# Attention, soft mixture of experts and MLP on one core: narrowing behind the copies, two pieces later, a reordered table of steps

## The chip, the cores and the metric

The kernel runs on one core of a Trainium2 chip. The metric is the device time of one launch in microseconds (us). Inputs lie in HBM: q, k, v of 4 batches, 12 heads, 448 positions and 64 channels; the experts' weights w1 and w2 (8 experts, 768 by 1024 and 1024 by 768, float32: 6.3 MB an expert); the weights w_in and w_out of the last MLP, which are float64 (768 by 2048 and 2048 by 768, 12.6 MB each).

## What is computed

```python
q_n, k_n = rmsnorm(q, g_q), rmsnorm(k, g_k)                 # per head
attn = softmax(q_n @ k_n.T / 8); x = attn @ v               # -> x: 1792 tokens x 768
logits = x @ phi                                            # 1792 x 32 slots, 4 slots per expert
d = softmax(logits, axis=0); slot_input = d.T @ x           # over tokens: 32 slots x 768
h = maximum(slot_input[e] @ w1[e], 0); slot_out[e] = h @ w2[e]      # 8 experts
c = softmax(logits, axis=1); x = c @ slot_out               # over slots, back to 1792 tokens
h = x @ w_in; g = maximum(h, 0) + alpha * minimum(h, 0); out = g @ w_out
```

## The kernel before, in words

**Attention** (to about 303 us). Two heads make a pair; 24 pairs are worked one behind the other with their steps interleaved. For each pair q and k are loaded, normed, split into two f16 parts, transposed on TensorE (L745) and copied out by ScalarE (L752). Four small transfers on SP's queue then arrange them: L754 and L756 copy k's and q's low parts into kB and qB, `twin` (L761) copies q's upper half over its lower one ("q<-q"), and L773 puts the negated row maximum into a row of qB ("qB<-mr"). `rowmax_mm` (L800) needs q before `twin` overwrites it; `score_mm` (L818) needs all four. ScalarE takes exp (L832, L834, L839), VectorE or GpSimd forms the low part (L850), and the matmuls of L868 and L878 multiply by v. In between, weights are fetched: "unit" is a buffer of 1.5 MB that holds half an expert's w1 or w2, or a raw piece of w_in; `pf` is the queue of such fetches (256 KB transfers at L475, 512 KB at L484), `cv` the queue of steps that narrow w_in from float64 to float32. All of it is 2374 steps in a list. A planner's due times do not set their order here: the table `ORDER` of 2374 numbers does (`plan = [plan[i] for i in ORDER]`, L1195). Each engine runs its own instructions in that order; SP's queue too is in order, a transfer that waits holds all behind it.

**Experts** (to about 417 us). For each expert e: its slot rows times w1[e] (L1339), a copy (`h_sb`, ScalarE, L1350), eight transposes (L1353), two short VectorE operations that write `hT` (L1355, L1361), then hT times w2[e] into the accumulators pS (L1370). In experts 2 to 5 `turn_c(e - 2)` follows: VectorE copies a batch's slot weights cN into `cs` (L1262), GpSimd forms their low part (L1263), TensorE transposes (L1267), ScalarE copies to cT4 (L1270). Expert 3 turns `alpha` ahead of that (L1252 to L1254).

The last 8 of w_in's 16 pieces are not yet narrowed when attention ends. `narrow_in(n)` does one: an absolute value on ScalarE (L540) and five VectorE operations (L541 to L551). `NARROW` says behind which expert which pieces stand.

The weights come as 32 units in a ring of 11 buffers, on SP's queue, w1 then w2 of each expert. Behind the 26th unit SP holds two transfers of w_out (`rawo` 0 and 1, L1281, 1.5 MB each, two pieces of w_out in each); they take the buffers of the two units of w2[5]. The last six units stand behind them. w_out's 16 pieces are widened by `wide_out(f)`: an absolute value (L498), four VectorE operations (L500 to L510), a cast to whi (ScalarE, L1301), a difference to wlo (VectorE, L1303). Pieces 0 to 3 are done early, in expert 6, by `go_early`; `EARLY_STEPS` is the order of their seven steps each. Behind piece 3 SP fetches `rawo` 5, then 2 and 3.

**Last MLP** (to the end). pS is copied out (`s_sb`, L1396: one half by VectorE, the other by ScalarE), turned and multiplied by w_in (L1402, L1414, L1442), and then TensorE runs three matmuls for each part of g times w_out (L1528 to L1530).

Of the kernel before, what the change touches and what calls it, by code (L numbers as in the profile page):

```python
# [353 lines left out]
def fused_attention_softmoe_mlp(  # L354
# [960 lines left out]
    def go_early():  # L1315
        for f in EARLY_STEPS:
            next(early[f], None)
# [5 lines left out]
    for e in range(E):  # L1323
# [38 lines left out]
        if e == E - 2:  # L1362
            go_early()
# [269 lines left out]
```

## Time and profile before

| | |
|---|---|
| median of 3 runs | 685.01 us (684.3 to 691.0) |
| the profiled execution | 685.3 us, span 683.3 us |
| TensorE busy | 616.2 us (90% of the span), mean granted clock 0.975 |
| VectorE, ScalarE, GpSimd busy | 464.9, 372.4, 191.6 us |
| HBM read | 92.18 MB |

The profile's span runs from the first to the last instruction; what lies around it is 2.0 us here. A busy TensorE is not one at its peak: matmuls are pipelined and their ends are modelled, so the waits and the distances between starts say more than the share.

### The profile page before, as it was taken

Reading aid. Unit: us, or ns where it says so; the run is one execution under the profiler, and the core shown is the slowest. Engines: PE = TensorE matmul, PEld = TensorE weight load, DVE = VectorE, ACT = ScalarE, POOL = GpSimd, SP = SyncE. Lnnn points to the kernel's source line nnn. Section 1 sums busy time; section 2 is a strip of 40 time slices with the busy share of each in tenths; the row PEclk is TensorE's granted clock in tenths of the full one; section 3 lists DMA queues with packets and bytes.
Section 4 is the critical chain, followed back from the end, with each engine's and each line's share of the span. In section 5 each row is a group of like instructions: output and inputs, shape, how many; then the busy total and the mean of one; then the engine's idle time right before and its main releaser. Section 6 shows DMA issues by size and latency. Waiting matters only on the chain.

```text
span 683.3 us, 14166 instructions
## 1 busy us (share of the span) xinstructions
PE 616.2 (90%) x5670; PEld 475.9 (70%) x5670; DVE 464.9 (68%) x921; ACT 372.4 (54%) x717; POOL 191.6 (28%) x203
## 2 busy tenths in 40 slices
PE   0799998989999999998868668999999999999997
PEld 0367665666667777764323214888899999999997
DVE  5788999998789877735941444999964545454540
ACT  3799998889999998742321223776521111111110
POOL 6976666557657764111001000000000000000000
PEclk9999999999999999999988969999999999999999
DMA  4575677364456325499999799130020101010101
GB/s 138 133 239 165 188 211 204 110 189 126 131 143 200 99 76 171 123 350 391 425 424 395 283 423 400 67 120 0 1 93 1 47 1 47 1 47 0 47 1 46
DMA packets 36240, 106.89 MB, mean 156 GB/s; under 512 B 5448, under 2 KB 22352, under 8 KB 31824
## 3 DMA queue, kind: packets, MB, share of 16 engines
q1 hardware_dynamic: 36176, 106.01, 44.7%
q8 instruction: 44, 0.72, 0.5%
q14 instruction: 20, 0.16, 0.1%
HBM read 92.18 MB, written 5.51 MB: 143 GB/s over the span
## 4 chain that ended last, share of the span: by engine, by line
PE 63%; ACT 14%; DMA 9%; DVE 8%; POOL 4%; issue 2%; SPq 1%; ACTq 0%; POOLq 0%; DVEq 0%
PE psa L1530 12%; PE psa L1529 12%; PE psa L1528 11%; PE psn L818 5%; DMA unit<-in_moe_w_dram 4%; PE psv L878 4%; PE psv L868 3%; PE psa L1339 3%; ACT e L834 3%; PE psr L800 2%; DMA q<-q 2%; ACT psn L839 2%; POOL nf L717 2%; PE psa L1370 2%; ACT sp L723 1%
## 5 line engine op out<-in xcount | busy, mean ns | idle before, releaser
L1528 PE MATMUL psa<-whi,gh 128*128 128x384 f32 (+1 forms) x448 | 152.0, 339 | 0.0
L1529 PE MATMUL psa<-wlo,gh 128*128 128x384 f32 (+1 forms) x448 | 151.1, 337 | 0.0
L1530 PE MATMUL psa<-whi,gl 128*128 128x384 f32 (+1 forms) x448 | 150.8, 337 | 0.0
L809 DVE TENSOR_REDUCE m<-psr 128x1 f16<-128x448 f32 x168 | 97.7, 615 | 4.8 <-PE psr L800 4.6
L1497 ACT CAST gh<-t 128x512 fp32r<-128x512 f32 x40 | 24.9, 621 | 123.0 <-DVE t L1494 122.5
L1529 PEld LDWEIGHTS psa<-wlo,gh 128*128 128x128 f32 x448 | 84.2, 188 | 2.7
L1528 PEld LDWEIGHTS psa<-whi,gh 128*128 128x128 f32 x448 | 84.2, 188 | 2.7
L1530 PEld LDWEIGHTS psa<-whi,gl 128*128 128x128 f32 x448 | 84.1, 188 | 2.8
L878 PE MATMUL psv<-vH,e 128*128 128x65 f16 (+1 forms) x1152 | 84.2, 194 | 0.0
L878 PEld LDWEIGHTS <-e 128*128 128x128 f16 (+1 forms) x1728 | 79.3, 106 | 0.0
L1491 DVE TENSOR_SCALAR t<-pst,alpha_t 128x256 f32<-128x256 f32 x80 | 34.9, 476 | 62.9 <-PE pst L1485 62.9
L868 PEld LDWEIGHTS psv<-vR,e 128*128 128x128 f32 (+1 forms) x384 | 58.9, 176 | 20.0 <-issue 10.8
L878 PE MATMUL psv<-vL,e 128*128 128x64 f16 (+1 forms) x576 | 72.5, 193 | 0.0
L850 POOL TENSOR_TENSOR e<-ef,e 128x448 f16<-128x448 f32 x48 | 52.0, 1083 | 72.2 <-ACT ef L839 52.7
L868 PE MATMUL psv<-vR,e 128*128 128x65 f32 (+1 forms) x384 | 69.8, 263 | 0.2 <-PE psn L818 0.2
L834 ACT ACTIVATE e<-psn 128x448 f16<-128x448 f32 x120 | 65.2, 544 | 7.5 <-PE psn L818 6.2
L818 PE MATMUL psn<-q,k 128*128 128x448 f16 (+1 forms) x192 | 61.4, 361 | 7.3 <-DMA q<-q 2.0
L818 PE MATMUL psn<-qB,kB 67*128 67x448 f16 (+1 forms) x192 | 61.0, 357 | 1.6 <-DMA qB<-mr 1.4
L800 PE MATMUL psr<-k,q 128*128 128x448 f16 (+1 forms) x192 | 57.2, 374 | 3.5 <-ACT k L752 2.8
L850 DVE TENSOR_TENSOR e<-psn,e 128x448 f16<-128x448 f32 x72 | 44.4, 617 | 21.4 <-ACT psn L839 21.2
L730 POOL TENSOR_TENSOR sp<-nf,sp 128x448 f16<-128x448 f32 x48 | 49.8, 1047 | 12.2 <-ACT sp L723 11.8
L745 PE MATMUL pst<-ident,sp 128*128 128x128 f16 x336 | 27.7, 230 | 17.4 <-POOL sp L730 17.4
(178 smaller groups left out, 1091.2 us busy)
## 6 DMA issues: line engine op xcount, KB each, us to landing
unit<-in_moe_w_dram SPq DMA_DIRECT2D x26, 1536.0 KB, 12.2
unit<-in_moe_w_in_dram SPq DMA_DIRECT2D x24, 512.0 KB, 6.8
rawo<-in_moe_w_out_dram SPq DMA_DIRECT2D x8, 1536.0 KB, 13.2
unit<-in_moe_w_dram SPq DMA_DIRECT2D x36, 256.0 KB, 4.9
qk<-in_q_dram SPq DMA_DIRECT2D x12, 448.0 KB, 3.8
qk<-in_k_dram SPq DMA_DIRECT2D x12, 448.0 KB, 5.4
out_dram<-osb SPq DMA_DIRECT2D x14, 384.0 KB, 2.3
vR<-in_v_dram SPq DMA_DIRECT2D x24, 128.0 KB, 3.8
```

The source lines that it names most:

```text
L730: eng.tensor_tensor(out=d["sp"][:, a, :, D:], in0=d["nf"][:, a], in1=d["sp"][:, a, :, 0:D], op=ALU.subtract)
L800: nc.tensor.matmul(pn[o0:o1, :S], d["q"][:, c0 : c0 + o1 - o0], d["k"][:, h * S : (h + 1) * S], start=True, stop=True)
L809: nc.vector.tensor_reduce(out=d["m"][:, c : c + 1], in_=d.pop(("pn", c))[:, :S], axis=AX.X, op=ALU.max)
L818: nc.tensor.matmul(pe[o0:o1, :S], lhs[:, c0 : c0 + o1 - o0], rhs[:, h * S : (h + 1) * S], start=st_, stop=not st_,)
L834: nc.scalar.activation(e2[:, 0], pe[:, :S], AF.Exp, scale=0.125)
L850: eng.tensor_tensor(out=e2[:, 1], in0=ef, in1=e2[:, 0], op=ALU.subtract)
L868: nc.tensor.matmul(pv[o0:o1, slot, :], d["e", c][:, qs], d["vv"][:, h, sl * D : 4 * D + 1], start=(j == 0), stop=False,)
L878: nc.tensor.matmul(pv[o0:o1, slot, 0:wd], d["e", c][:, w // 2, qs], (vl if w == 1 else vh)[:, 4 * h + sl, 0:wd], start=(j == 0 and w == 0) ...
L1491: nc.vector.tensor_scalar(out=t0[:, cs], in0=ph[:, cs], scalar1=0.0, scalar2=alpha_t[:, f // 2, i : i + 1], op0=ALU.min, op1=ALU.mult)
L1528: nc.tensor.matmul(a, gh[f][:, ms], hi[:, hs], start=(f == 0 and not (packed and m % 2 == 1 and hf == 0)), stop=False)
L1529: nc.tensor.matmul(a, gh[f][:, ms], lo[:, hs], start=False, stop=False)
L1530: nc.tensor.matmul(a, gl[f][:, ms], hi[:, hs], start=False, stop=(f == KF - 1 and not (packed and m % 2 == 0 and hf == 1)))
```

## The change

Three things. The narrowing of w_in's pieces stands behind `turn_c` and not ahead of the second matmuls, and piece 15 goes from expert 3 to expert 4. `EARLY_STEPS` is in two parts, one in expert 6, one in expert 7: pieces 0 and 1 and the start of 2 in the first, the rest of 2 and all of 3 in the second. The table `ORDER` is another one from its 500th step on, which is the fifth pair's; it holds the same 2374 steps.

```diff
@@ ORDER, from its 500th number on
-    244, 1462, 2002, 2003, 1655, 268, 222, 318, 292, 2198, 52, 1679, 1227, 364, 978, 1084, 438, 1607, 923, 2199, 2200,
...
+    244, 1462, 2002, 1679, 558, 2198, 268, 1227, 364, 1829, 1486, 1251, 222, 1607, 318, 582, 2199, 1084, 1132, 978,
...
@@ -1310,16 +1310,19 @@
-    EARLY_STEPS = [0, 1, 0, 0, 0, 0, 0, 2, 1, 1, 1, 1, 0, 1, 3, 2, 2, 2, 2, 1, 2, 3, 3, 3, 3, 2, 3, 3]
-
-    def go_early():
-        for f in EARLY_STEPS:
+    EARLY_STEPS = (
+        (0, 1, 0, 0, 0, 0, 1, 1, 1, 1, 0, 0, 2, 1, 1, 2, 2, 2, 2),
+        (2, 3, 2, 3, 3, 3, 3, 3, 3),
+    )
+
+    def go_early(part):
+        for f in EARLY_STEPS[part]:
             next(early[f], None)
...
-    NARROW = ((8, 9), (10, 11), (12, 13), (14, 15), (), (), (), ())
+    NARROW = ((8, 9), (10, 11), (12, 13), (14,), (15,), (), (), ())
...
@@ -1359,10 +1362,8 @@
-        if e == E - 2:
-            go_early()
-        for n in NARROW[e]:
-            narrow_in(n)
+        if e >= E - 2:
+            go_early(e - E + 2)
         for u in range(2):
             wu = loaded[1, e, u].rearrange("p (t f) -> p t f", t=4)
...
         if 2 <= e < 2 + B:
             turn_c(e - 2)
+        for n in NARROW[e]:
+            narrow_in(n)
```

Three lines are added above the experts' code, so what was L1339 is L1342 in the changed kernel, L1350 and L1353 are L1353 and L1356, L1355 is L1358, L1396 is L1399.

What the change moves, in the engines' own order. On VectorE at the end of expert 2, the kernel before (the second of the two pieces, the casts of cN, then expert 3's hT; L1262 is the cast that `turn_c` waits for):

```order
L541 TENSOR_SCALAR wf<-wf 128x768
L543 CAST wb<-low 128x768
L545 TENSOR_SCALAR wf<-wf 128x768
L548 SCALAR_TENSOR_TENSOR wf<-wb,wf 128x768
L551 SCALAR_TENSOR_TENSOR win_4271<-win_4271,wf 128x768
L1262 CAST cs<-cN 128x4x32 x2
L1355 TENSOR_REDUCE hT<-pst 128x4x4
```

The same place in the changed kernel (expert 2's hT, the casts, then the first of the two pieces):

```order
L1358 TENSOR_REDUCE hT<-pst 128x4x4
L1364 TENSOR_SCALAR hT<-hT 128x4x4
L1262 CAST cs<-cN 128x4x32 x2
L541 TENSOR_SCALAR wf<-wf 128x768
L543 CAST wb<-low 128x768
L545 TENSOR_SCALAR wf<-wf 128x768
L548 SCALAR_TENSOR_TENSOR wf<-wb,wf 128x768
L551 SCALAR_TENSOR_TENSOR win_4231<-win_4231,wf 128x768
```

The casts come ahead of the narrowing, and the narrowing now stands ahead of the next expert's hT. On ScalarE, the absolute values move behind `turn_c`'s copy in the same way.

On VectorE in expert 7, the kernel before (the end of w_out's piece 3, the differences of pieces 2 and 3, then hT; L1396 is the copy of pS with which the last MLP begins):

```order
L506 SCALAR_TENSOR_TENSOR wf<-rawo,wf 128x768
L510 SCALAR_TENSOR_TENSOR wf<-rawo,wf 128x768
L1303 TENSOR_TENSOR wlo<-wf,whi 128x768 x2
L1355 TENSOR_REDUCE hT<-pst 128x4x4
L1361 TENSOR_SCALAR hT<-hT 128x4x4
L1355 TENSOR_REDUCE hT<-pst 128x4x4
L1361 TENSOR_SCALAR hT<-hT 128x4x4
L1396 COPY s_sb<-psa 128x384
```

The same place in the changed kernel (from the second half of hT on; L1399 is that copy):

```order
L1358 TENSOR_REDUCE hT<-pst 128x4x4
L1364 TENSOR_SCALAR hT<-hT 128x4x4
L1303 TENSOR_TENSOR wlo<-wf,whi 128x768
L500 TENSOR_SCALAR wf<-wf 128x768
L502 TENSOR_SCALAR wf<-wf 128x768
L506 SCALAR_TENSOR_TENSOR wf<-rawo,wf 128x768
L510 SCALAR_TENSOR_TENSOR wf<-rawo,wf 128x768
L1303 TENSOR_TENSOR wlo<-wf,whi 128x768
L1399 COPY s_sb<-psa 128x384
```

Expert 7's hT was behind all four pieces, and so was its h_sb on ScalarE, behind their casts (L1301). Now piece 2's cast and difference and all of piece 3 stand behind hT and ahead of s_sb.

On SP's queue at the end of attention, before (qB_117 belongs to the last pair):

```order
L773 DMA qB_115<-mr 1x7x128
L475 DMA unit<-in_moe_w_dram 128x512
L761 DMA q<-q 64x896
L773 DMA qB_117<-mr 1x7x128
L475 DMA unit<-in_moe_w_dram 128x512 x12
```

and now:

```order
L773 DMA qB_115<-mr 1x7x128
L659 DMA vR_124<-in_v_dram 64x2x256
L475 DMA unit<-in_moe_w_dram 128x512 x10
L761 DMA q<-q 64x896
L475 DMA unit<-in_moe_w_dram 128x512
L773 DMA qB_117<-mr 1x7x128
L475 DMA unit<-in_moe_w_dram 128x512
```

The last pair's `twin` had one 256 KB transfer between itself and the pair's before it; it now has ten.

## Rows read from the trace of the kernel before

**Rows 1.** Windows: us, busy us (instructions) by engine, granted clock, DMA share, GB/s.
```profile
90.00:303.00 213.00, 203.07 (x2727) 149.14 (x2726) 174.28 (x363) 188.35 (x391) 121.33 (x120) 1.00 0.54 158
320.00:340.00 20.00, 18.37 (x164) 7.35 (x163) 18.98 (x38) 6.77 (x10) 0.00 (x0) 1.00 1.01 428
480.00:520.00 40.00, 40.00 (x232) 37.15 (x232) 28.56 (x48) 14.16 (x24) 0.00 (x0) 1.00 0.11 40
```

**Rows 2.** Windows around the hole in the transfers, same columns.
```profile
374.00:376.00 2.00, 2.00 (x22) 0.59 (x15) 0.00 (x0) 0.58 (x1) 0.00 (x0) 1.00 0.33 131
...
374.00:382.00 8.00, 7.95 (x72) 3.29 (x68) 1.06 (x6) 1.75 (x3) 0.88 (x2) 1.00 0.21 56
```

**Rows 3.** Waits of SP's queue, 370 to 386: total us, times, longest.
```profile
SPq L1281 <- PE psa L1370: 15.4, 2, 14.5
```

**Rows 4.** Timeline, experts 0 to 2: start, us, engine, line, idle before and releaser.
```profile
320.84 0.55 DVE L541 TENSOR_SCALAR wf<-wf 128x768 f32<-128x768 f32 x1
...
326.77 0.96 DVE L551 SCALAR_TENSOR_TENSOR win<-win,wf 128x768 uint32<-128x768 uint32 x1
...
335.73 2.79 PE L1370 MATMUL psa<-unit,hT 128*32 128x384 f32 x32
...
344.29 1.20 PE L1267 MATMUL pst<-ident,cs 128*128 128x128 f32 x4 [5.77 <-POOL cs L1263]
```

**Rows 5.** Timeline, experts 3 to 6.
```profile
345.42 6.03 PE L1339 MATMUL psa<-unit,slT 128*32 128x512 f32 x24
345.52 0.97 ACT L1270 CAST cT<-pst 128x448 fp32r<-128x448 f32 x1 [5.98 <-PE pst L1267]
...
360.09 0.17 DVE L1253 COPY alpha_t<-pst 128x16 f32<-128x16 f32 x1
...
362.82 5.86 PE L1339 MATMUL psa<-unit,slT 128*32 128x512 f32 x24
...
369.40 0.22 DVE L1355 TENSOR_REDUCE hT<-pst 128x16 f32<-128x64 f32 x1 [8.66 <-PE pst L1353]
...
370.09 2.79 PE L1370 MATMUL psa<-unit,hT 128*32 128x384 f32 x32
...
373.49 3.62 PE L1339 MATMUL psa<-unit,slT 128*32 128x512 f32 x24
...
378.51 2.79 PE L1370 MATMUL psa<-unit,hT 128*32 128x384 f32 x32
...
380.07 1.62 SPq L1281 DMA_DIRECT2D rawo<-in_moe_w_out_dram  x2
```

**Rows 6.** Timeline, expert 7 and the copy behind it.
```profile
405.98 1.91 PE L1339 MATMUL psa<-unit,slT 128*32 128x512 f32 x12 [0.97 <-DMA unit<-in_moe_w_dram]
...
407.59 0.56 DVE L500 TENSOR_SCALAR wf<-wf 128x768 f32<-128x768 f32 x1 [0.99 <-ACT wf L498]
...
409.77 0.96 DVE L510 SCALAR_TENSOR_TENSOR wf<-rawo,wf 128x768 uint32<-128x768 uint32 x1
410.65 1.94 DVE L1303 TENSOR_TENSOR wlo<-wf,whi 128x768 fp32r<-128x768 f32 x2
410.76 0.83 ACT L1301 CAST whi<-wf 128x768 fp32r<-128x768 f32 x1 [2.48 <-DVE wf L510]
411.50 1.07 ACT L1350 COPY h_sb<-psa 128x512 f32<-128x512 f32 x2
...
412.13 1.98 PE L1353 MATMUL pst<-ident,h_sb 128*128 128x128 f32 x8 [4.24 <-ACT h_sb L1350]
...
416.79 0.56 DVE L1396 COPY s_sb<-psa 128x384 f32<-128x384 f32 x1 [2.20 <-PE psa L1370]
```

**Rows 7.** Window at expert 7's transposes, columns as in group 1.
```profile
412.00:414.00 2.00, 1.87 (x8) 1.58 (x8) 0.98 (x3) 0.57 (x2) 0.00 (x0) 0.50 0.96 406
```

**Rows 8.** Timeline, first widening step of w_out's piece 4.
```profile
428.29 0.92 ACT L498 ACTIVATE wf<-rawo 128x768 f32<-128x768 f32 x1
```

**Rows 9.** Waits of TensorE in attention, 90 to 303: total us, times, longest.
```profile
PE psn L818 <- DMA q<-q: 1.6, 1, 1.6
```

184 rows, old and new, of the table ORDER are left out of this document.

## The prediction, before the changed kernel was run

> **What bounds the kernel now.** I read the windows by stage first, then the waits of SP's queue, then the timeline of the experts, where the change's second and third parts lie. From 428 us on TensorE has no gap (40.00 of 40 us in 480 to 520 [rows 1]), so the last MLP is a block that ends earlier by as much as it begins earlier. Ahead of it the experts' stage runs at the rate of the transfers: a DMA share of 1.01 at 428 GB/s [rows 1], by which a 1.5 MB piece takes 3.7 us. But there is one hole. The share is 0.33 in 374 to 376, so the queues run dry at 374.7, and 0.21 over 374 to 382 [rows 2]: 8 x 0.79 = 6.3 us lost. SP waited there, 15.4 us in all, for expert 5's L1370 [rows 3], whose weights' buffers the two pieces of w_out take; six pieces of the experts' weights stand behind these two. They were issued at 380.07, 1.56 us after that L1370 began at 378.51 [rows 5], and began to flow some 0.9 us later (a share of 0.21 over 8 us is 1.7 us of work: 0.7 ahead of the hole, the rest from 381.0 on). So the hole ends when TensorE has reached expert 5's second matmuls, and TensorE is late there: it idles 5.77 us ahead of `turn_c` in expert 2 [rows 4], because the casts of cN stand behind two narrowed pieces on VectorE, and again in expert 3; L1339 then takes 6.03 and 5.86 us where it takes 3.62 in expert 5 [rows 5].
>
> **Part 1, the narrowing behind the copies.** I walk TensorE from expert 2's L1370, at 335.73 [rows 4]. Where nothing waits, L1370 to the next expert's L1339 takes 373.49 - 370.09 = 3.4 us with `turn_c` in it, and L1339 to its own L1370 takes 378.51 - 373.49 = 5.0 [rows 5].
> - Expert 3's L1339: 335.7 + 3.4 = 339.1, not 345.42.
> - Behind it ScalarE runs L1270 (0.97, beginning 0.1 after L1339 [rows 5]) and the absolute value (another pass over 128x768, for which I take the cast's 0.83 [rows 6]), and VectorE two pieces, 320.84 to 327.73 = 6.9 us [rows 4]. Only then comes expert 3's hT, and L1370 begins 0.7 after hT does (369.40, 370.09 [rows 5]): 339.1 + 1.9 + 6.9 + 0.7 = 348.6. Of the 5.0 us cover 4.5 us are overrun; this is where a part of the gain is given back.
> - Expert 3 has alpha to turn ahead of the casts: L1370's 2.79, two small matmuls (0.4, an estimate), then 2.7 from the copy of alpha to L1339 (360.09, 362.82 [rows 5]): expert 4's L1339 at 354.5, not 362.82.
> - One piece in expert 3, one in expert 4: 1.9 + 3.45 + 0.7 = 6.1 us from L1339 to L1370. Expert 4's L1370 at 360.6, expert 5's L1339 at 364.0, its L1370 at 370.1, not 378.51: 8.4 us earlier.
>
> Transfers allow this pace: the unit that lands at 374.7 is the second half of w1[6], so at 3.7 us each the last one that expert 5 needs has landed by 367.3.
>
> **Part 1's effect, the hole.** The two pieces of w_out are issued at 370.1 + 1.56 = 371.7 and flow at 372.6, 2.1 us ahead of the moment at which the queues run dry. The hole closes, and every later landing comes 6.3 us earlier. The 2.1 us are the margin; what the walk is late beyond it is left of the hole, one for one.
>
> **Part 2, w_out's pieces 2 and 3 later.** In expert 7 the second half of L1339 began on a landing, at 405.98, and ended at 407.89; h_sb came only at 411.50, behind piece 3's cast at 410.76 [rows 6]. Now: landing 399.7, L1339's end 401.6, and no cast of piece 3 ahead of h_sb. In expert 5, where nothing was ahead, L1370 began 378.51 - (373.49 + 3.62) = 1.4 us after L1339's end; that is behind hT's first half, and for the second (one operation of 0.22 [rows 5] and a shorter one) I add 0.5: hT at 403.5. VectorE then does piece 2's difference (0.97), piece 3's four operations (407.59 to 410.73 = 3.14), and after the cast's 0.83 its difference (0.97) [rows 6]: 5.9 us, to 409.4, and the copy of pS, which was at 416.79, begins there. The last matmuls are not what it waits for: eight pieces of 3.7 us from 381.0 on land by 410.6, 6.3 earlier by 404.3, and 2.8 us of matmuls behind it end at 407.1. So VectorE's tail replaces the landing as the last to come. **Gain 416.8 - 409.4 = 7.4 us.** Were the tail free, TensorE's 407.1 would give 9.7; were the transposes at the lower clock as in 412 to 414 (granted 0.50 [rows 7]; L1353 took 1.98 [rows 6], half of which would be the clock's), it would be 6.4.
>
> **The clock behind it.** TensorE idles from 407.1 to 410.0 ahead of the last MLP's first matmuls, where there was next to no gap before. After an idle time of 0.97 us the matmuls ran at full speed (1.91 us for half of what takes 3.62), after 4.24 us the granted clock was 0.50 [rows 5 to 7], the lower of its two levels; 2.9 us lies between. The Trainium skill (TensorE: Matmul & The Clock Gate, section Part 1: The HAM clock gate) makes the low clock the default that activity releases, so by it an idle stretch is paid for behind it as well, and this speaks against moving piece 3 ahead of s_sb: by the rule in full the sum would be -5.9, without it -7.4; the trace agrees with it as far as 412 to 414 go. From the rows alone: if the clock falls, the first 3 us of the chain run at half speed (from 412.13 to 415 it did so), which costs at most 1.5; I take the middle, 0.8, and keep 0 and 1.5 as ends.
>
> **What is hidden.** Piece 15 in expert 4 is in the walk. `rawo` 5 is now issued behind piece 3's L510, at 407.7; `rawo` 4 keeps the queues busy until 404.3 + 3.7 = 408.0, so at worst half a microsecond is lost, and `rawo` 2, two pieces later, lands by 416.4 where its first use, at 428.29 [rows 8] and 7 us earlier now, comes at 421. Fetches and widening behind that move with the block.
>
> **The attention's new order.** It removes and adds no instruction; the rows of one pair are in other places by a few microseconds either way. From 90 to 303 us TensorE idles 213 - 203.07 = 9.9 us and ScalarE 24.7 [rows 1]; so at best some 10 us go. The longest single wait there is 1.6 us, of L818 for q<-q [rows 9]. At one place the order speaks against it: the last pair's `twin` stands behind ten 256 KB transfers, 6.1 us at 428 GB/s. Its first use in TensorE's order lies two matmul groups later than before, and before there was room, so I count 0 to 3 us there. For the other pairs I see no direction: 0, with -5 (half of TensorE's idle time) and +5 (the last pair's 3 and one more 1.6 us wait) as ends.
>
> **Sum.** -7.4 + 0.8 + 0 = -6.6: the profiled execution's 685.3 becomes 678.7. The median is 685.0, 0.3 lower, so **678.4 us**. About 1% (6.9 us) is what a measurement of this kernel can tell from no change; the forecast lies on that edge.
>
> **Rivals.**
> - *The order of attention gains too.* For it: 9.9 us of idle TensorE, and ScalarE, which takes 188 of 213 us, has room. Against it: the waits are many and short. Half of the idle time gone gives 678.4 - 5 = 673.4.
> - *The hole stays.* The narrowing now delays each hT, and the margin is 2.1 us. If expert 5's L1370 comes hardly earlier than its 378.5, landings do not move and only expert 7's queue is shorter: L1339's end at 407.9, hT at 409.8, s_sb at 415.7 and not 416.8, so 1.1 us less what the clock takes: 684.3. Against it: the waits of 5.8 us ahead of `turn_c` are certain to go.
> - *Slower: the four small transfers come late in attention.* The new order sets q<-q or mr behind weight transfers as at the last pair, L818 waits at each such pair, and TensorE stands, since it is in order. At 1.6 us each [rows 9] the gain is eaten when 5 of the 20 reordered pairs wait, and the kernel is over 1% slower from 9 on: 8 of them give 678.4 + 12.8 = 691.2. Against it: the kernel before has one such wait for q<-q in 213 us.
> - *The parts do not add up*: pieces 2 and 3 do not stand behind hT in fact. That can be excluded from VectorE's order above.
>
> **Chances and range.** Forecast 0.56, attention gains 0.24, hole stays 0.11, slower 0.09. The forecast's own range is 675.5 to 681.5 (the clock's and transposes' bounds and some 2 us of attention). 8 in 10 lie in 672.5 to 684: the low end takes in the first rival, the high end most of the second. Faster by over 1% (below 678.1): 0.45 of the forecast's chance (0.25) and the first rival's (0.24), 0.49. Slower by over 1% (above 691.9): less than half of the third rival's, 0.04. Within 1%: the rest, 0.47.
>
> **What would show it.** The waits of L1267 for `cs` in experts 2 and 3 fall below 1 us (expert 3 keeps the turn of alpha); a wait of L1353 or L1370 behind narrowing appears instead. L1339 takes 3.6 us in experts 3 and 4. `rawo` 0 is issued before the queues are dry, and no window from 320 us to the last landing has a share far below 1. The copy of pS waits for VectorE's own queue, not for TensorE. The span to the first L1339 tells the order's part apart from the rest. The forecast is wrong if that moves by more than 3 us, or if a second hole opens behind piece 3's late fetch.

## The result, and the profile after

| | kernel before | changed kernel |
|---|---|---|
| median of 20 runs each | 688.92 us (684.3 to 693.8) | 682.02 us (678.5 to 691.1) |
| ratio | 1 | 0.9902 (95%: 0.988 to 0.9924), 5.2 to 8.3 us less |
| the profiled execution | 685.3 us, span 683.3 us | 680.28 us, span 678.4 us |

The change makes the kernel 1.0% faster. The forecast was 678.4 us, 6.6 below its base of 685.01; 688.92 - 682.02 is 6.9. The base was the median of the first three of the 20 runs; over all 20, and over three later groups of 17 to 35 runs, the kernel before has medians of 687.98 to 688.92 us. So the change was forecast within half a microsecond, and the level 3.6 us too low.

Lines of the changed kernel are numbered 3 higher than before from L1339 on (L1342, L1353, L1356, L1358, L1399, L1405); only L1370 becomes L1371.

The windows of the changed kernel (us, busy us and instructions by engine, granted clock, DMA share, GB/s), to be held against [rows 1, 2]:

```profile
374.00:376.00 2.00, 2.00 (x28) 0.78 (x24) 0.32 (x3) 0.00 (x0) 0.88 (x2) 1.00 1.04 436
374.00:382.00 8.00, 6.98 (x61) 2.07 (x53) 0.32 (x3) 1.57 (x2) 0.88 (x2) 1.00 1.02 429
...
480.00:520.00 40.00, 40.00 (x235) 37.82 (x235) 27.85 (x49) 12.18 (x21) 0.00 (x0) 1.00 0.10 40
```

The share over 374 to 382 is 1.02 where it was 0.21: the hole is closed. The last MLP is the same block, 261.80 us from its L1405 to the last matmul and 261.79 before.

The timeline of the changed kernel, experts 2 to 6 (start, us, engine, line, idle time before and what ended it), the counterpart of [rows 4, 5]:

```profile
341.51 0.75 PE L1267 MATMUL pst<-ident,cs 128*128 128x128 f32 x4
...
342.19 3.62 PE L1342 MATMUL psa<-unit,slT 128*32 128x512 f32 x24
...
347.24 1.05 ACT L1353 COPY h_sb<-psa 128x512 f32<-128x512 f32 x2
...
347.86 1.24 PE L1356 MATMUL pst<-ident,h_sb 128*128 128x128 f32 x8 [2.05 <-ACT h_sb L1353]
...
349.89 0.96 DVE L551 SCALAR_TENSOR_TENSOR win<-win,wf 128x768 uint32<-128x768 uint32 x1
...
350.77 0.22 DVE L1358 TENSOR_REDUCE hT<-pst 128x16 f32<-128x64 f32 x1
...
351.25 4.22 PE L1371 MATMUL psa<-unit,hT 128*32 128x384 f32 x32 [2.15 <-DVE hT L1364]
...
357.42 1.05 PE L1267 MATMUL pst<-ident,cs 128*128 128x128 f32 x4 [1.62 <-POOL cs L1263]
...
358.40 4.91 PE L1342 MATMUL psa<-unit,slT 128*32 128x512 f32 x24
...
364.72 2.79 PE L1371 MATMUL psa<-unit,hT 128*32 128x384 f32 x32
...
373.76 2.79 PE L1371 MATMUL psa<-unit,hT 128*32 128x384 f32 x32 [0.55 <-DVE hT L1364]
...
375.32 1.62 SPq L1281 DMA_DIRECT2D rawo<-in_moe_w_out_dram  x2
...
380.10 1.91 PE L1342 MATMUL psa<-unit,slT 128*32 128x512 f32 x12 [1.02 <-DMA unit<-in_moe_w_dram]
```

In expert 2 L1267 no longer waits; in expert 3, where alpha is turned first, it still waits 1.62 us (5.72 before). In place of these waits come those that the forecast named: h_sb behind the second absolute value, hT behind the second piece's L551, 2.05 and 2.15 us. The next L1342, expert 4's, takes 4.91 us, not the 3.6 that the forecast had for experts 3 and 4. Expert 5's L1371 starts at 373.76, not 378.51, and `rawo` 0 is issued at 375.32.

Expert 7 and the copy behind it, the counterpart of [rows 6, 7]:

```profile
403.44 0.59 ACT L1353 COPY h_sb<-psa 128x512 f32<-128x512 f32 x1 [2.94 <-PE psa L1342]
...
409.81 1.50 PE L1371 MATMUL psa<-unit,hT 128*32 128x384 f32 x16 [2.19 <-DMA unit<-in_moe_w_dram]
...
410.96 0.96 DVE L1303 TENSOR_TENSOR wlo<-wf,whi 128x768 fp32r<-128x768 f32 x1 [0.90 <-ACT whi L1301]
411.36 0.48 ACT L1399 COPY s_sb<-psa 128x384 f32<-128x384 f32 x1 [0.44 <-PE psa L1371]
411.83 0.55 DVE L1399 COPY s_sb<-psa 128x384 f32<-128x384 f32 x1
412.43 1.41 PEld L1405 LDWEIGHTS pst<-stack,s_sb 128*128 128x128 f32 x12 [1.82 <-DVE s_sb L1399]
412.44 1.52 PE L1405 MATMUL pst<-stack,s_sb 128*128 128x32 f32 x12 [1.13 <-DVE s_sb L1399]
```

h_sb comes at 403.44, right behind its matmuls and no longer behind a cast. VectorE's copy of pS starts at 411.83, 4.96 us earlier than [rows 6] show, behind piece 3's L1303; ScalarE's half, which waits for TensorE alone, at 411.36.

**Where 4.9 us of span came from.** Expert 0 shows that the two profiles do not start level. Kernel before, then changed kernel:

```profile
315.42 3.62 PE L1339 MATMUL psa<-unit,slT 128*32 128x512 f32 x24 [0.45 <-DVE slT L1229]
```
```profile
316.93 5.16 PE L1342 MATMUL psa<-unit,slT 128*32 128x512 f32 x24 [0.45 <-DVE slT L1229]
```

It starts 1.5 us later and takes 1.5 us longer. To see whose doing that is, I set four marks in every profile of this study: the 575th matmul (up to it TensorE's order, by line and tile, is the same in all of them), the first L1222, the start of expert 0's second matmuls (L1370 or L1371), and the last MLP's first matmul (L1402 or L1405). All in us:

| profile | 575th matmul at | to L1222 | expert 0's second matmuls at | from there to expert 5's | from there to the last MLP | from it to the last matmul |
|---|---|---|---|---|---|---|
| before | 76.10 | 236.56 | 320.39 | 58.12 | 97.01 | 261.79 |
| changed | 77.68 | 236.50 | 323.45 | 50.32 | 88.99 | 261.80 |
| e1_moe_only (old order) | 77.61 | 237.48 | 326.03 | 50.99 | 89.97 | 264.76 |
| e2_order_only | 76.82 | 240.53 | 325.31 | 56.38 | 94.43 | 261.79 |
| e3_twin | 78.29 | 236.90 | 324.59 | 50.38 | 89.02 | 261.81 |
| e4_old_early | 76.15 | 237.93 | 323.21 | 50.24 | 90.75 | 261.79 |
| e5_wf3 | 77.62 | 239.32 | 326.37 | 50.65 | 88.43 | 265.33 |
| e6_rawpos (old order) | 78.19 | 240.00 | 327.61 | 56.72 | 91.24 | 261.79 |
| e8_both | 77.03 | 236.08 | 324.04 | 44.49 | 86.78 | 261.74 |
| e9_idle | 77.56 | 237.29 | 322.79 | 50.37 | 91.67 | 264.81 |
| e10_late_only (old order) | 77.10 | 239.22 | 327.24 | 57.07 | 95.23 | 265.46 |
| e11_fill | 77.55 | 239.20 | 326.12 | 45.16 | 87.77 | 261.79 |
| e12_old_order (old order) | 77.12 | 237.25 | 322.19 | 45.57 | 87.83 | 261.75 |
| e13_fill2 | 77.16 | 237.45 | 324.70 | 44.96 | 87.85 | 261.79 |

The span's -4.9 is then: +1.58 up to the 575th matmul, -0.06 in the attention, +1.54 at expert 0 (its clock), -8.02 in the experts, 0 behind them.

### The profile page after: what moved, and what is told of

It reads as the page before. It is cut to its first block, busy times and chain, and to the rows that moved or that the text cites. A ratio compares the mean times of both kernels' runs of the same rounds, so it can differ in the third digit from the quotient of the medians.

```text
span 678.4 us, 14149 instructions
## 1 busy us (share of the span) xinstructions
PE 616.3 (91%) x5670; PEld 472.3 (70%) x5670; DVE 470.6 (69%) x921; ACT 374.7 (55%) x717; POOL 197.8 (29%) x203
## 4 chain that ended last, share of the span: by engine, by line
PE 65%; DVE 17%; ACT 6%; DMA 5%; POOL 3%; issue 2%; SPq 0%; DVEq 0%; POOLq 0%; ACTq 0%
PE psa L1532 12%; PE psa L1533 12%; PE psa L1531 12%; PE psn L818 5%; PE psv L878 4%; PE psv L868 4%; DMA unit<-in_moe_w_dram 4%; DVE m L809 3%; PE psr L800 3%; PE psa L1342 2%; PE psa L1371 2%; PE pst L745 2%; DVE e L850 1%; PE pst L1488 1%; POOL nf L717 1%
## 5 line engine op out<-in xcount | busy, mean ns | idle before, releaser
L800 PE MATMUL psr<-k,q 128*128 128x448 f16 (+1 forms) x192 | 58.6, 379 | 5.4 <-ACT k L752 2.8
L730 POOL TENSOR_TENSOR sp<-nf,sp 128x448 f16<-128x448 f32 x48 | 53.6, 1128 | 6.9 <-ACT sp L723 6.5
L745 PE MATMUL pst<-ident,sp 128*128 128x128 f16 x336 | 29.1, 233 | 17.6 <-POOL sp L730 17.4
```

Of the source, the lines that this page charges most:

```text
L730: eng.tensor_tensor(out=d["sp"][:, a, :, D:], in0=d["nf"][:, a], in1=d["sp"][:, a, :, 0:D], op=ALU.subtract)
L745: nc.tensor.transpose(blocks[:, b0 : b1 + 1 : b1 - b0], d["sp"][:, a, c], ident16)
L800: nc.tensor.matmul(pn[o0:o1, :S], d["q"][:, c0 : c0 + o1 - o0], d["k"][:, h * S : (h + 1) * S], start=True, stop=True)
```

## The experiments

Each ratio is the time of a run's kernel over that of the kernel before, run beside it, with the 95% interval in brackets.

**The experts' edits alone (e1).** The edit: the changed kernel with the old numbers in `ORDER`.

> The kernel before with the experts' edits alone (narrowing behind turn_c, piece 15 in expert 4, w_out's pieces 2 and 3 in expert 7); the attention keeps its old order. Theory: these edits give the whole gain and the new order takes some of it back (in the one profile of the changed kernel the first L1342 comes 1.5 us later than the old one, 316.93 and 315.42). Then the first L1342 is at 315.4 as before, no window from 326 us on has a DMA share far below 1, the second half of expert 7's L1342 comes 6.3 us earlier than 405.98, and the ratio to the kernel before is 0.988 to 0.990 (8.2 to 6.7 us less). Rival 1, the order gives a part: the ratio is 0.992 to 0.995. Rival 2, the hole is not closed by the edits but by the other order, which would bring expert 5's matmuls earlier: the hole stays in the trace and the ratio is 0.998.

Measured: 0.991 (0.9875 to 0.9945). In its trace expert 5's second matmuls stand 50.99 us behind expert 0's and not 58.12; between 372 and 384 us the only thin window is 380 to 382, with a share of 0.75. The second half of expert 7's L1342 comes 6.9 us earlier by the same count (78.66 and 85.59). So the experts' edits close the hole without the new order; rival 2 falls. The first L1342 was expected at 315.4 and came at 318.42, later than in the changed kernel: the later start is not the new order's doing. The interval takes in the theory's range and rival 1's, so the time does not tell these two apart. The profile, that of one of the three slowest of 12 runs (686.7 us), also shows what the forecast had priced too low. TensorE idles longer ahead of L1405 here (start, us, idle before; then two windows):

```profile
415.40 0.55 DVE L1399 COPY s_sb<-psa 128x384 f32<-128x384 f32 x1
...
416.00 2.77 PE L1405 MATMUL pst<-stack,s_sb 128*128 128x32 f32 x12 [2.32 <-DVE s_sb L1399]
```
```profile
416.00:422.00 6.00, 6.00 (x43) 4.32 (x44) 0.32 (x2) 0.61 (x2) 0.00 (x0) 0.50 1.00 428
422.00:424.00 2.00, 2.00 (x19) 0.77 (x18) 0.52 (x2) 0.37 (x1) 0.00 (x0) 0.80 1.03 426
```

The granted clock is 0.50, the lower of its two levels, for over 6 us, and the last MLP takes 264.76 us instead of 261.8: 3 us.

**The order alone (e2).** The edit: the kernel before with the new numbers in `ORDER`.

> The kernel before with the new order of the attention alone; the experts as before. Theory: the last pair's second copy of q behind ten 256 KB pieces makes L818 wait for q<-q again, some 1.7 us at 291 to 293, and the first L1339 comes 1 to 2 us later than 315.42; the hole at 374 to 381 stays, moved by as much; ratio 1.001 to 1.003. Rival 1, the order gains (TensorE's many short waits fall): the first L1339 by 313 or earlier, ratio 0.993 to 0.997. Rival 2, no effect beyond one profile's scatter: 0.999 to 1.001.

Measured: 0.9968 (0.9937 to 0.9999), 0.1 to 4.3 us less. The wait for q<-q is there, 1.9 us, the hole stays (shares of 0.09 and 0.00 from 380 to 384), and the first L1339 came at 320.34; but its 240.53 us in the attention are hardly above what the four other kernels with the old order took (237.25 to 240.00), and the time is not longer. The theory falls in its sign; of the rivals' ranges, the first (0.993 to 0.997) lies in the interval, though the first L1339 by 313 that belongs to it did not come, and the second (0.999 to 1.001) reaches into it.

**The last pair's second copy earlier (e3).** The edit moves one number of `ORDER`:

```diff
-    ..., 549, 335, 2084, 599, ...    ...  2096, 406, 1363, 2334, ...
+    ..., 549, 335, 1363, 2084, 599, ...   ...  2096, 406, 2334, ...
```

By it two of the last pair's seven row-maximum products (L800) read q after the copy, which alters the maximum that is taken off the exponent.

> The changed kernel, with the last pair's second copy of q issued ahead of the ten 256 KB pieces instead of behind them; nothing else is moved. Theory: the wait of 1.66 us of L818 for q<-q goes, the first L1342 comes 1.5 us earlier (315.4, was 316.93), and with it everything behind: ratio to the kernel before 0.988 where the changed kernel has 0.9902. Rival 1: L818 then waits for the next late thing at that place (the row mr, or ScalarE's e), and the first L1342 moves by less than 0.5 us: 0.990. Rival 2: the wait goes, but the experts run at the rate of the transfers and the first expert's start does not count: the start moves and the last landing doesn't, 0.990.

Measured: 0.9924 (0.9891 to 0.9956). TensorE's waits, 276 to 300 us, changed kernel and then e3:

```profile
292.98 0.36 PE L818 MATMUL psn<-q,k 128*128 128x448 f16 x1 [1.66 <-DMA q<-q]
```
```profile
285.04 0.36 PE L800 MATMUL psr<-k,q 128*128 128x448 f16 x1 [1.26 <-DMA q<-q]
...
294.19 0.35 PE L818 MATMUL psn<-qB,kB 67*128 67x448 f16 x1 [0.73 <-DMA qB<-mr]
```

One wait of 1.66 us became two of 1.99 in sum: the row-maximum products now wait for the copy, and the next late row is mr. That is rival 1; the attention took 236.90 us, 236.50 without the edit.

**Without the edit on w_out's pieces (e4).** The edit puts the old `EARLY_STEPS` and the one call back:

```diff
-        if e >= E - 2:
-            go_early(e - E + 2)
+        if e == E - 2:
+            go_early()
```

> The changed kernel without the edit on w_out's pieces: all four are narrowed in expert 6 again, in the old sequence of steps, ahead of h_sb and hT of expert 7. Theory (the prediction's step, with the landing as the trace of the changed kernel has it): the hole stays closed, ScalarE reaches h_sb of expert 7 only behind the cast of piece 3, some 3.6 us behind L1342's end, and s_sb comes 1.5 to 3.6 us later than 411.4 to 411.8; ratio 0.992 to 0.995. Rival 1: landings are 3.7 us earlier and so are the pieces, piece 3 ends in the shadow of the wait for the last weights, and nothing changes: 0.990. Rival 2: TensorE's clock falls behind the longer idle time too, another 1 us: 0.996.

Measured: 0.997 (0.9933 to 1.0007), some 4.7 us (1.7 to 7.7, from the two intervals) more than the changed kernel. The hole stays closed. TensorE's longest wait between 400 and 415 us:

```profile
PE pst L1353 <- ACT h_sb L1350: 5.1, 1, 5.1
```

h_sb stands behind piece 3's cast again, and the last MLP starts 1.76 us later, counted from expert 0's second matmuls. From there to the end it takes the same 261.79. The ratios differ by more than these 1.76 us, and the granted clock of each run points to why: 7 of the 12 runs have a mean of 0.952 to 0.964 and take 684.8 to 690.6 us, the other five, the profiled one among them, 0.970 to 0.976 and 681.2 to 685.7; in the changed kernel 3 of 20 are that low. The sign and the wait are the theory's; the size is nearer to rival 2, the clock (0.996), though no trace shows where it fell in the slower runs.

**Three wf buffers (e5).** The edits:

```diff
-    wfs = (hp, 2)
+    wfs = (hp, 3)
-        (0, 1, 0, 0, 0, 0, 1, 1, 1, 1, 0, 0, 2, 1, 1, 2, 2, 2, 2),
-        (2, 3, 2, 3, 3, 3, 3, 3, 3),
+        (0, 1, 0, 0, 0, 0, 1, 1, 1, 1, 2, 2, 2, 2, 2, 0, 0, 1, 1, 2, 2),
+        (3, 3, 3, 3, 3, 3, 3),
```

and `bufs=3` for both wf tiles of `narrow_in`.

> The changed kernel with three buffers of wf instead of two, so that w_out's piece 2 gets its four operations on VectorE while the casts of pieces 0 and 1 wait for the weights' buffers (VectorE is idle for 7.0 us there, 390.9 to 397.9 in the trace of the changed kernel), and only piece 3 is left for expert 7. Theory: VectorE's tail (piece 3's L1303 ends at 411.9, together with TensorE's L1371) no longer decides when s_sb is copied, in no execution; the copy comes right behind the last L1371, TensorE's idle time ahead of L1405 stays below 1.2 us, and the slower clock behind it (which the run with the old order of the attention had: idle 2.3 us, granted clock 0.50 for 7 us, 2.96 us more from L1405 to the end) goes. Median 1 to 2 us below the changed kernel: ratio to the kernel before 0.987 to 0.989, and fewer executions above 686. Rival: TensorE and the landing end together with VectorE anyway, and the slow executions come from elsewhere: 0.990, with as many above 686.

Measured: 0.9903 (0.9871 to 0.9934), which takes in the theory's 0.988 and the rival's 0.990; two of its 12 runs at 686 or above. VectorE's tail is shorter, but piece 3's L1303 still ends with TensorE's last matmuls, and its profile, that of the slowest of the 12, shows the slow clock all the same, from an idle time one step earlier:

```profile
412.29 2.58 PE L1371 MATMUL psa<-unit,hT 128*32 128x384 f32 x16 [2.20 <-DVE wf L510]
...
414.80 2.77 PE L1405 MATMUL pst<-stack,s_sb 128*128 128x32 f32 x12
```

The 2.20 us are the wait for the last weights (the changed kernel has 2.19 at that place, put down to the transfer). Behind it the clock fell here and did not fall there. So the theory's "in no execution" falls: the tail is not the only place that costs the clock.

**w_out's fetch two pieces later, old narrowing (e6).**

```diff
-    "RAWPOS": 26,
+    "RAWPOS": 28,
```

> The kernel before with one number changed: the first two pieces of w_out are fetched two weight pieces later in SP's queue; narrowing and the attention as before. Theory: the hole at 374.7 to 381 is there only because these two pieces wait for expert 5's L1370 ahead of the others; with two more weight pieces (7.4 us) ahead of them the queues have work until 382, past the 380.07 at which they are issued, and the hole closes with no edit of the narrowing. The second half of expert 7's L1339 then comes 6.3 us and two pieces (7.4 us) earlier for the experts' own weights, w_out's pieces later by the same; s_sb comes 3 to 6 us earlier than 416.8, ratio 0.991 to 0.996. Rival 1: another piece waits for a buffer at that place and the hole stays: 0.999. Rival 2: w_out's later pieces put their narrowing behind everything and the end comes later: 1.002 or more.

Measured: 0.9959 (0.993 to 0.9988). The hole is gone although narrowing and attention are those of before and expert 5's L1370 came at 384.33; window, SP's issue and TensorE's longest wait for ScalarE between 400 and 420:

```profile
374.00:382.00 8.00, 7.95 (x69) 3.40 (x68) 1.06 (x6) 1.90 (x3) 0.88 (x2) 1.00 1.03 429
```
```profile
385.89 1.62 SPq L1281 DMA_DIRECT2D rawo<-in_moe_w_out_dram  x2
```
```profile
PE pst L1353 <- ACT h_sb L1350: 4.9, 1, 4.9
```

So the hole is what the forecast said: pieces in line behind two that wait for a buffer. Expert 7's second half of L1339 comes 7.1 us earlier, counted from expert 0's second matmuls (78.5 and 85.6); the expectation had two pieces, 7.4 us, more, but expert 7's w1 still stands behind w_out's two. The last MLP comes only 5.8 earlier (91.24 and 97.01): h_sb waits behind w_out's narrowing again.

**Three buffers and one piece to an expert (e8).**

```diff
-    NARROW = ((8, 9), (10, 11), (12, 13), (14,), (15,), (), (), ())
+    NARROW = ((8, 9), (10, 11), (12,), (13,), (14,), (15,), (), ())
```

on top of e5's edits.

> The run with three wf buffers, and w_in's pieces 12 to 15 narrowed one to an expert (behind turn_c of experts 2 to 5) instead of two, one, one. Theory: the waits of L1356 and L1371 behind narrowing in expert 3 (2.15 and 2.05 us in the changed kernel's trace) go, w_out's first pieces are issued some 3 us earlier, but the queues were never dry, so the landings do not move: ratio as the run with three wf buffers, 0.987 to 0.989. Rival: the margin (about 1 us between issue and dry queues in the changed kernel) is used up in some executions, so the median falls another 0.5 to 1 us: 0.986 or less. Other rival: a piece in expert 5 delays its hT and the issue: 0.991.

Measured: 0.9875 (0.9836 to 0.9915). Expert 5's second matmuls come 5.8 us earlier than in the changed kernel (44.49 against 50.32), `rawo` 0 is issued at 370.09, and the last MLP starts 2.2 us earlier (86.78, 88.99). The last weights are used 1.4 us earlier by the same count (84.97, 86.36), where the theory let the landings stand. The time agrees with the theory and with its first rival; its interval and the changed kernel's overlap, so it is not shown to be faster.

**A longer idle time (e9).**

```diff
+    for _ in range(2):
+        nc.vector.tensor_tensor(out=s_sb, in0=win[0][:, :DM], in1=win[0][:, DM : 2 * DM], op=ALU.subtract)
```

> The changed kernel with two operations over 128x768 added on VectorE between the end of the narrowing and the copy of pS (their result is overwritten), 1.9 us by L1303's duration. TensorE then idles 3.0 us ahead of L1405 where it idled 1.13. Theory: the clock falls behind that idle time, L1405 takes 2.8 instead of 1.5 us, and from L1405 to the end it takes 264.8 instead of 261.8 us; together 4.9 us more than the changed kernel, ratio 0.997. Rival 1 (the prediction's size): the fall costs 0.8 to 1.5: 3 us more, 0.9945. Rival 2: the clock does not fall: 1.9 more, 0.993.

Measured: 0.9962 (0.9929 to 0.9996), by the two ratios 4.1 us more than the changed kernel. Its profile:

```profile
411.80 1.94 DVE L1399 TENSOR_TENSOR s_sb<-win 128x768 f32<-128x768 f32 x2
...
414.46 2.23 PE L1407 MATMUL pst<-stack,s_sb 128*128 128x32 f32 x12 [3.17 <-DVE s_sb L1401]
```

The copies come 2.0 us later, and the last MLP takes 264.81 us, 3.0 more: 5.0 in all. In this profile the theory holds, and the forecast's size of 0.8 (0 to 1.5) does not; the interval of the times lies about the theory's 0.997 but takes in both rivals too.

**The edit on w_out's pieces alone (e10).** The kernel before with the two-part `EARLY_STEPS`.

> The kernel before with the edit on w_out's pieces alone (0 to 2 in expert 6 and the rest in expert 7, behind its hT); narrowing of w_in and the attention as before. Theory: the hole stays, since nothing ahead of expert 5's L1370 is changed; h_sb of expert 7 no longer waits for piece 3's cast (3.6 us in the kernel before), but VectorE then has piece 3 ahead of the copy of pS, so that of the 3.6 us only 1 to 2 come back: ratio 0.997 to 0.999. Rival 1: all 3.6 us come back, 0.995. Rival 2: VectorE's tail makes TensorE idle over 2 us ahead of L1402 and the clock falls, 3 us more: 1.001 to 1.003.

Measured: 1.0026 (1.0000 to 1.0051). The hole stays, and moves (share in 382 to 386):

```profile
382.00:386.00 4.00, 3.95 (x37) 1.85 (x36) 1.07 (x6) 1.17 (x2) 0.88 (x2) 1.00 0.00 0
...
424.00:430.00 6.00, 6.00 (x40) 3.29 (x40) 0.68 (x2) 0.61 (x2) 0.00 (x0) 0.50 1.01 430
```
```profile
419.84 2.12 PE L1373 MATMUL psa<-unit,hT 128*32 128x384 f32 x16 [2.21 <-DMA unit<-in_moe_w_dram]
...
422.46 2.77 PE L1405 MATMUL pst<-stack,s_sb 128*128 128x32 f32 x12 [0.51 <-DVE s_sb L1399]
```

The last MLP starts 1.8 us earlier (95.23, 97.01) and takes 3.7 us longer (265.46), at the clock of 0.50. The time and the clock are rival 2's, the wait is not: VectorE's tail leaves 0.51 us ahead of L1405, and the 2.21 us stand ahead of the last weights' matmuls. This is the slowest of the 12 runs (693.97 us); where the 1.8 us went in the others is not shown. In the kernel before TensorE's long idle time (4.24 us [rows 6]) lies ahead of transposes that take some 0.5 us more for it (1.98; 1.50 in e10), and 3.3 us of matmuls follow without a gap; here the wait stands close ahead of the dense last MLP.

**Transposes in the last wait (e11).** Six transposes of the identity between the halves of expert 7's last matmuls, on top of e8.

> The run with three wf buffers and one piece to an expert, with six transposes of the identity (never read) on TensorE between the two halves of expert 7's last matmuls, where it waits 2.2 us for the last weights. Theory: the executions with 3 us more and a granted clock of 0.95 to 0.96 come from the clock's fall in these last waits; with TensorE kept at work for 1.1 of the 2.2 us it no longer falls, executions above 684 disappear, and the median is 0 to 1.5 us below the run without them: ratio 0.986 to 0.9875. Rival 1: the fill does not keep the clock, nothing changes, 0.9875. Rival 2: the transposes take longer than the wait and delay the last matmuls: 0.989.

Measured: 0.9901 (0.9863 to 0.994), one of 6 runs above 684. The wait fell from 2.2 to 1.40 us and the clock held in this profile, as it had in e8's without the transposes. The interval takes in the theory and both rivals; nothing here shows that the transposes helped.

**Old order, best experts (e12).** e8 with the old numbers in `ORDER`.

> The run with three wf buffers and one piece to an expert, with the old order of the attention. Theory: the new order of the attention is worth nothing either way (from the last matmul that both orders share, at 76 us, to the first L1222 it took 236.50 us in the changed kernel and 236.56 in the kernel before): same median as with the new order, ratio 0.986 to 0.989. Rival 1: the new order gains some 2 us, as the run with the new order alone (0.9968) would have it: 0.990 to 0.992. Rival 2: it loses: 0.985 or less.

Measured: 0.9899 (0.987 to 0.9929), e8 0.9875; the intervals overlap. It takes in most of the theory's range (0.986 to 0.989) and all of rival 1's (0.990 to 0.992), and the measured ratio lies between them: undecided.

**Transposes ahead of expert 0 too (e13).** Eleven more, ahead of L959, L974, L1007 and L1222.

> The run with the six transposes, and eleven more of them in TensorE's short waits between the attention and the first expert (3, 3, 2 and 3, in the waits of 0.5 to 0.7 us ahead of L959, L974, L1007 and L1222). Theory: the clock's fall between 311 and 321 us, which 8 of 9 profiles of changed kernels show and the profile of the kernel before does not (its first L1339 took 3.62 us, theirs 5.0 to 6.3), comes from these waits; filled, L1222 and the first L1342 run at full speed, expert 0's L1371 comes 1.5 to 2.7 us earlier and, the transfers being what bounds the experts, the end too by as much: ratio 0.9825 to 0.985. Rival 1: the clock falls all the same, 0.9865. Rival 2: the transposes delay the waiting operations more than the clock gives: 0.988.

Measured: 0.991 (0.9882 to 0.9937). The clock fell all the same:

```profile
311.00:317.00 6.00, 4.46 (x75) 3.99 (x67) 2.53 (x12) 1.14 (x2) 0.00 (x0) 0.82 1.01 423
317.00:321.00 4.00, 3.55 (x18) 0.95 (x20) 0.36 (x1) 0.00 (x0) 1.81 (x1) 0.50 0.32 135
```
```profile
313.11 0.31 PE L1017 MATMUL pst<-X,dn 128*32 128x128 f32 x3 [1.39 <-DVE run L1042]
```

But the run does not test the theory. The transposes shortened the waits that they stand in, and a new one of 1.39 us came in the middle of L1017 (L1007 before), where e8 has none: from 302 to 326 us TensorE's waits add up to 3.00 us, in e8 to 2.89. The time lies above rival 1's 0.9865 and rival 2's 0.988. (The count in the expectation was wrong: in e2, e9 and e12 the first expert's matmuls also ran in 3.62 us, the fall having come earlier, at L1222.) What brings this fall is left open.

## Why the prediction was right, point by point

**Part 1, the walk.** Counted from expert 0's second matmuls, expert 5's were forecast at 370.1 - 320.4 = 49.7 us; they came at 50.32 and in the kernel before at 58.12. The pieces of the walk fit too, each within 1.1 us by that count: the overrun of 4.5 us in expert 3 is the 2.05 and 2.15 us of waits. What the walk did not have is a slow L1371 (4.22 us) and L1342 (4.91) behind those waits.

**Part 1's effect.** Shown: the hole closes with part 1 (e1, e4), and for the reason given (e6). Expert 7's second half of L1342 starts at 402.33, 78.88 us behind expert 0's second matmuls, where it was 85.59: 6.7 earlier, forecast 6.3.

**Part 2.** The mechanism is shown (e4, e6: h_sb waits 5 us behind the cast when the pieces stand ahead of it). But the forecast had no term for how the two parts hang together. Alone, part 1 with the new order gives 2.1 us (e4, 0.997) and part 2 gives none or loses up to 3.5 (e10); together, with the old order, 6.2 (e1). Closing the hole brings the landing forward, and then the casts decide; moving the casts alone leaves the hole. The rival "the hole stays" gave part 2 alone a gain of 1.1 us less the clock's cost (its 684.3 takes 0.4 for that, half of the sum's 0.8); e10 shows no gain.

**What ends last.** The forecast let VectorE's tail end 2.3 us behind TensorE. It ended last: the copy of pS was forecast 89.0 us behind expert 0's second matmuls and came at 88.38. But it ended last by 0.5 us only, since the landings had been put too early. In the changed kernel the matmuls at 380.10 and at 409.81 wait for weights eight pieces apart; 29.7 us lie between them, 3.71 a piece, as forecast; but the forecast let a piece be usable when its share of the rate had flowed. In the kernel before, three pieces of 3.7 us from 381.0 on end, by this estimate, at 392.1, and the matmuls that wait for the third begin 2.0 later (its timeline):

```profile
394.07 2.77 PE L1370 MATMUL psa<-unit,hT 128*32 128x384 f32 x14 [7.06 <-DMA unit<-in_moe_w_dram]
```

The Trainium skill (DMA: Bandwidth & Descriptors, section Anatomy of one DMA) states a fixed 2.0 us for a transfer on another path than this one, most of it between the last byte and the semaphore; the row agrees.

**The clock.** This term was mis-sized. It was +0.8, at most 1.5, on the ground that the first 3 us run at half speed. In the profiled execution it was 0: TensorE idled 1.13 us and not 2.9, and the granted clock behind it was 1.00. It was not 0 in every run: 3 of the changed kernel's 20 have a mean granted clock of 0.953 to 0.958 and take 688.0 to 691.1 us, the others 0.970 to 0.985 and 678.5 to 683.6. Where a profile shows the fall at the last MLP it cost 3.0 (e1, e9) to 3.7 us (e5, e10), since the 0.50 lasted over 6 us of dense matmuls. By the Trainium skill (TensorE: Matmul & The Clock Gate, section Part 1: The HAM clock gate) the low clock is the default and activity releases it, so a fall is paid for by the work behind the idle time; e9 agrees, at 3.0 us for 2.0 us more of idle time.

**The attention.** Forecast 0, and the marks give -0.06 between the two profiles. With the old order the attention took 236.56, 237.48, 240.00, 239.22 and 237.25 us, median 237.5; with the new one (without e13) 236.08 to 240.53, median 237.6. The last pair's wait, put at 0 to 3 us, is 1.66. In the times all three pairs of kernels lean to the new order (0.9902 and 0.991; 0.9968 and 1; 0.9875 and 0.9899), by 0.5 to 2.2 us, each at or within its interval; whether it gains a microsecond stays open.

**The level.** 685.3 us was a good execution of the kernel before: expert 0's matmuls ran at full speed and the 575th matmul stood at 76.10, where the other profiles have 76.15 to 78.29. The sum against it was right for the change and 3.6 us too low for the median. That -6.6 meets the medians' -6.9 so closely is in part luck: in the two profiles the experts gave 8.0 us, 0.6 more than the sum's 7.4, and the clock took nothing where the sum had 0.8, while the medians hold slower runs of both kernels.

## What to carry to other kernels

A queue in order that runs dry has two remedies: let the work that frees the buffer come earlier (part 1), or let what does not need the buffer go ahead (e6, one number). Either shows its whole gain only when the next thing in line, here the casts ahead of h_sb, moves too; so price such edits together, and test each alone before crediting it. An idle time cost most here directly ahead of a dense block of matmuls: 2 us more of it cost 5 in e9's profile.

## What the runs showed of the hardware that was not expected

- TensorE's clock: idle times of 2.2 us ahead of the last weights were followed by 0.50 in e5 and e10 and by 1.00 in the changed kernel, e3, e8, e9 and e12; so the length of one idle time alone does not tell.
- Between 311 and 325 us the clock fell to 0.50 in 13 of the 14 profiles, for 3 to 10 us, behind gaps of 0.5 to 0.7 us between matmuls; only the profile of the kernel before has no such fall, and it has the same gaps. Whether they bring it is open, since e13 left the sum of the waits about as it was.
- The same matmuls, up to the 575th, took 76.1 to 78.3 us: a profile can stand 2 us off its neighbour before the edit has begun.
